# Normalized q and k transposed by a DMA from SBUF to SBUF, in place of TensorE transposes and a PSUM copy

## The chip, the cores and the metric

The kernel runs on one core of one Trainium2 chip. A core has five engines that run side by side: TensorE (PE in the profile; its weight loads are listed as PEld), VectorE (DVE), ScalarE (ACT), GpSimd (POOL) and SyncE (SP). Each works through its own instructions in a fixed order and waits on semaphores for the others. Here SP does nothing but issue DMA transfers, which 16 DMA engines carry out. SBUF is the working memory with 128 partitions, PSUM the memory into which TensorE writes.

The metric is the device time of one execution in microseconds (us); lower is better.

## The reference

Cosine attention, followed by a highway layer on its output:

```python
batch, n_heads, seq, head_dim = (8, 12, 448, 64)      # d_model = 768

q_n = q / (np.linalg.norm(q, axis=-1, keepdims=True) + 1e-06)
k_n = k / (np.linalg.norm(k, axis=-1, keepdims=True) + 1e-06)
scores = np.matmul(q_n, k_n.transpose(0, 1, 3, 2)) / tau          # tau = 0.1
scores = scores - np.max(scores, axis=-1, keepdims=True)
attn = np.exp(scores)
attn = attn / (np.sum(attn, axis=-1, keepdims=True) + 1e-09)
attn_out = np.matmul(attn, v)

x = attn_out.transpose(0, 2, 1, 3).reshape(B * S, H * D)          # 3584 x 768
H = np.maximum(x @ w_h, 0.0)
T = 1.0 / (1.0 + np.exp(-(x @ w_t + b_t)))
out = T * H + (1.0 - T) * x
```

## The kernel before

Work is cut into 8 batches of 6 pairs of heads. A pair's 448 rows lie on 112 partitions in 4 chunks; `(b,pr)` below is batch b, pair pr. For a pair the steps are these.

- `emit_A` loads q and k (two transfers of 224 KB, SP), squares them on POOL (`qk_sq`, L97) and sums the squares on DVE (L104).
- `emit_rsqrt` makes the inverse norms `yy` on DVE with eleven small operations, for batch 0 pair by pair and later for a whole batch at once.
- `emit_B` multiplies q and k by them on POOL (`qkn`, two instructions, L152), transposes `qkn` so that the head dimension lies on the partitions (`qkT`, eight blocks on PE, L157), copies the result from PSUM to SBUF on DVE (`qkt`, L164), loads v, and casts it to fp16 on ACT into `vp` (L174), whose last column POOL sets (the memset, L173).
- `emit_qkt` computes the scores (`sT`, L186) from `qkt`, and ACT takes their exponentials (`expt`, L194).
- `emit_av`, for each head, multiplies by v (`u`, 16 matmuls, L208); DVE divides by the row sums (`rd`, `xbach`, L219 and L220).

The highway layer of the batch before is spread over the heads of the current one (`ffn_slot`): a transpose of x on PE (`xTp`, L234), the two products (`pt`, L255), and the elementwise end on ACT and DVE, with one store for each of 4 row chunks. The last batch's layer runs alone at the end.

The code is not run in the order in which it is written. A scheduler sets the order on each engine from the dependences and from the order of writing, which gives each step its priority; `tc.high_priority(offset=300)` moves a step ahead. In the written order `emit_A(b+1, ...)` stands in the first six heads of batch b and `emit_B(b+1, ...)` in the last six. All of batch 0's pairs and the loads of the weights come first.

What holds a step back besides its inputs is a free buffer: 7 for `qk_raw`, 4 each for `qkn`, `qkt`, `vp` and `expt`, 3 for `v_raw`, and 2 PSUM buffers, tagged `pb1`, which `qkT`, `u` and `xTp` share. The weights' fp32 buffer exists once, so the load of `w_t` waits until DVE has cast `w_h` (L76).

Of the kernel before, what the change touches and what calls it, by code (L numbers as in the profile page):

```python
# [10 lines left out]
FP16 = mybir.dt.float16  # L11
# [7 lines left out]
def kernel(  # L19
# [11 lines left out]
    nc = tc.nc  # L31

    B, NH, S, D = q.shape
    P = 112
    NC = S // P
# [14 lines left out]
    qt_p = ctx.enter_context(tc.tile_pool(name="qt", bufs=4))  # L50
# [9 lines left out]
    pb1_p = ctx.enter_context(tc.tile_pool(name="pb1pool", bufs=2, space=bass.MemoryType.PSUM))  # L60
    ffnp_p = ctx.enter_context(tc.tile_pool(name="ffnpool", bufs=2, space=bass.MemoryType.PSUM))

    ident = const.tile([P, P], FP16)
# [82 lines left out]
    def emit_B(b, pr):  # L146
        qk_raw = st.pop(("qk_raw", b, pr))
        rs = st["rs", b].rearrange("p (pr t c h) -> p pr t c h", pr=NPAIR, t=2, c=NC)
        qkn = qkn_p.tile([128, 2, NC, 2, D], FP16, name="qkn")
        for t in range(2):  # L150
            in1 = rs[:P, pr, t].unsqueeze(3).to_broadcast([P, NC, 2, D])
            nc.gpsimd.tensor_mul(qkn[:P, t], qk_raw[:P, t], in1)  # L152

        qkT = pb1_p.tile([128, 2, 512], FP16, name="qkT", tag="pb1")
        for t in range(2):
            for c in range(NC):
                nc.tensor.transpose(  # L157
                    qkT[:, t, c * P : (c + 1) * P],
                    qkn[:P, t, c],
                    ident[:P, :P],  # L160
                )
        qkt = qt_p.tile([128, 2, S], FP16, name="qkt")
        with tc.high_priority(offset=300):
            nc.vector.tensor_copy(qkt[:, :, :], qkT[:, :, 0:S])  # L164
        st["qkt", b, pr] = qkt

        v_raw = vraw_p.tile([128, NC, 2, D], FP32, name="v_raw")
        nc.sync.dma_start(
            v_raw[:P],
            v[b, 2 * pr : 2 * pr + 2].rearrange("h (p c) d -> p c h d", c=NC),  # L170
        )
        vp = vp_p.tile([128, NC, 2, D + 1], FP16, name="vp")
        nc.gpsimd.memset(vp[:P, :, :, D], 2.0)  # L173
        nc.scalar.copy(vp[:P, :, :, 0:D], v_raw[:P])  # L174
        st["vp", b, pr] = vp
# [139 lines left out]
    for pr in range(NPAIR):  # L315
        emit_A(0, pr)
        emit_rsqrt(0, prs=pr)
        emit_B(0, pr)
# [11 lines left out]
    for b in range(B):  # L330
        for h in range(NH):
            pr, hh = h // 2, h % 2
            if b + 1 < B and h < NPAIR:
                emit_A(b + 1, h)
            if hh == 0:
                for h2 in (h, h + 1):
                    st["expt", b, h2] = expt_p.tile([128, NC, S], FP16, name="expt")
                emit_qkt(b, pr, 0)
                emit_qkt(b, pr, 1)
            emit_av(b, h)  # L340
            if b >= 1:
                ffn_slot(b - 1, h)
            if b + 1 < B and h >= NPAIR:
                if h == NPAIR:
                    emit_rsqrt(b + 1)
                    new_batch_tiles(b + 1)
                emit_B(b + 1, h - NPAIR)
# [6 lines left out]
_INS = ['q', 'k', 'v', 'tau', 'moe_w_h', 'moe_w_t', 'moe_b_t']  # L354
_OUTS = [((3584, 768), 'float32')]
#: Inputs that are plain numbers.
_NUMBERS = {'tau': 0.10000000149011612}


# [26 lines left out]
```

## Time and profile before

| | us |
|---|---|
| median of 2 runs | 512.3 |
| lowest and highest | 511.74 and 512.85 |
| span of the profiled execution (first to last instruction) | 509.7 |
| the profiled execution's busy times: PE, DVE, ACT, POOL | 412.6, 314.3, 226.1, 201.7 |
| mean granted TensorE clock, as a share of full speed | 0.887 |

The busy times overlap, since the engines run side by side, so they don't add up to the span. A PE busy time counts from a matmul's start to its modelled end, with overlapping matmuls counted once. In rows of instructions the first number is the start in us from the span's start, the second the length, then engine, line, operation, the tile written and the tile read, shapes, count, and in brackets the idle time before and what ended it. In rows of groups the numbers after the bar are the busy time in us and the mean length in ns. The granted clock is what the throttle allowed TensorE.

### The profile page before, as it was taken

What the parts mean: (1) busy time and instruction counts of PE and PEld (TensorE: products, weight loads), DVE (VectorE), ACT (ScalarE), POOL (GpSimd) and SP (SyncE); (2) the same over time, 40 slices, a digit from 0 to 9 for tenths busy, and PEclk for the clock granted to TensorE, in tenths of its full rate; (3) what the DMA queues carried; (4) which work ended last, traced back from release to release, by engine and by line L of the source; (5) the groups of instructions that cost most, each with busy time, mean ns of one, the idle gap of its engine ahead of it and who ended that gap; (6) DMA issues with size and microseconds to landing.
All of it is one profiled execution on the core that took longest, in us unless ns stands there. A gap on an engine that the chain in (4) does not pass through costs nothing.

```text
span 509.7 us, 8460 instructions
## 1 busy us (share of the span) xinstructions
PE 412.6 (81%) x3328; PEld 286.6 (56%) x3328; DVE 314.3 (62%) x661; ACT 226.1 (44%) x305; POOL 201.7 (40%) x198
## 2 busy tenths in 40 slices
PE   0545945988776979889878999989887999899995
PEld 0114604766554656557655666657564767575774
DVE  3655465458277675666777494938685455453574
ACT  1321441346335453354453473454546455644511
POOL 3663296723924276337170833282517030000000
PEclk9999999999967797677898797959897899797999
DMA  9960695725553157415551554255231221000012
GB/s 173 224 167 1 211 192 105 147 57 129 109 117 81 39 131 140 100 46 113 142 110 45 132 123 103 62 118 138 70 74 46 64 65 46 27 28 28 29 55 81
DMA packets 137033, 49.31 MB, mean 97 GB/s; under 512 B 131873, under 2 KB 131873, under 8 KB 136994
## 3 DMA queue, kind: packets, MB, share of 16 engines
q1 hardware_dynamic: 136994, 48.77, 42.9%
q8 instruction: 26, 0.43, 0.4%
q14 instruction: 13, 0.11, 0.1%
HBM read 37.75 MB, written 11.01 MB: 96 GB/s over the span
## 4 chain that ended last, share of the span: by engine, by line
PE 53%; DVE 23%; ACT 5%; POOL 5%; SPq 5%; DMA 4%; issue 3%; POOLq 0%; ACTq 0%
PE pt L255 24%; PE u L208 15%; PE sT L186 9%; DVE outst L299 6%; DVE th1a L291 6%; DVE n L104 4%; PE qkT L157 4%; POOL qkn L152 3%; ACT expt L194 3%; SPq L92 3%; DMA qk_raw<-in_k_dram 3%; ACT tt L271 2%; DMA qk_raw<-in_q_dram 2%; POOL qk_sq L97 2%; DVE xTb L240 1%
## 5 line engine op out<-in xcount | busy, mean ns | idle before, releaser
L194 ACT ACTIVATE expt<-sT 112x896 f16<-112x896 f32 x192 | 166.7, 916 | 96.5 <-PE sT L186 77.7
L208 PEld LDWEIGHTS <-expt 112*112 112x112 f16 x1536 | 115.5, 158 | 40.1 <-issue 17.4
L208 PE MATMUL u<-vp,expt 112*112 112x65 f16 x1536 | 121.5, 238 | 12.9 <-DVE xbach L220 9.2
L255 PEld LDWEIGHTS <-xTb 128*112 128x112 f16 x768 | 101.8, 145 | 47.8 <-DVE xTb L240 15.0
L152 POOL TENSOR_TENSOR qkn<-qk_raw,yy 112x512 f16<-112x512 f32 x96 | 99.7, 1068 | 72.4 <-DVE yy L144 37.7
L186 PE MATMUL sT<-qkt 64*112 64x448 f16 x384 | 104.3, 437 | 26.3 <-ACT expt L194 25.6
L97 POOL TENSOR_TENSOR qk_sq<-qk_raw 112x1024 f16<-112x1024 f32 x48 | 96.3, 2013 | 29.5 <-DMA qk_raw<-in_k_dram 23.3
L255 PE MATMUL pt<-w_h_f,xTb 128*112 128x384 f16 x384 | 100.0, 402 | 5.4 <-DVE xTb L240 4.4
L174 ACT CAST vp<-v_raw 112x512 f16<-112x512 f32 x48 | 29.8, 621 | 118.8 <-PE u L208 78.8
L255 PE MATMUL pt<-w_t_f,xTb 128*112 128x384 f16 x384 | 77.2, 330 | 0.4 <-DVE hmx L274 0.3
L104 DVE TENSOR_REDUCE n<-qk_sq 112x16 f16<-112x1024 f16 x48 | 58.0, 1211 | 26.2 <-POOL qk_sq L97 26.2
L291 DVE SCALAR_TENSOR_TENSOR th1a<-tt,hmx 112x384 f16<-112x384 f16 x64 | 51.1, 798 | 33.2 <-ACT tt L271 33.2
L157 PE MATMUL qkT<-ident,qkn 112*128 112x112 f16 x384 | 35.5, 247 | 44.2 <-POOL qkn L152 40.9
L186 PEld LDWEIGHTS <-qkt 64*112 64x112 f16 x384 | 31.2, 140 | 62.3 <-issue 55.4
L173 POOL MEMSET vp<- 112x8 f16 x48 | 6.9, 149 | 147.4 <-PE u L208 147.4
L274 DVE SCALAR_TENSOR_TENSOR hmx<-pt,xbach 112x384 f16<-112x384 f32 x64 | 35.2, 553 | 39.2 <-PE pt L255 39.2
L271 ACT ACTIVATE tt<-pt 112x384 f16<-112x384 f32 x64 | 31.4, 491 | 62.6 <-PE pt L263 62.0
L157 PEld LDWEIGHTS <-qkn 112*128 112x128 f16 x384 | 28.5, 116 | 54.5 <-POOL qkn L152 45.7
L219 DVE RECIPROCAL rd<-u 112x4 f32<-112x4 f32 x96 | 17.2, 179 | 55.3 <-PE u L208 54.4
L299 DVE SCALAR_TENSOR_TENSOR outst<-xbach,th1a 112x384 f32<-112x384 f16 x64 | 49.2, 769 | 1.0
L164 DVE COPY qkt<-qkT 128x896 f16<-128x896 f16 x48 | 29.8, 620 | 21.1 <-PE qkT L157 11.8
L220 DVE SCALAR_TENSOR_TENSOR xbach<-u,rd 112x256 f16<-112x256 f32 x96 | 40.3, 421 | 1.9
(55 smaller groups left out, 116.8 us busy)
## 6 DMA issues: line engine op xcount, KB each, us to landing
qk_raw<-in_q_dram SPq DMA_DIRECT2D x48, 224.0 KB, 4.4
qk_raw<-in_k_dram SPq DMA_DIRECT2D x48, 224.0 KB, 4.4
v_raw<-in_v_dram SPq DMA_DIRECT2D x48, 224.0 KB, 3.4
out_dram<-outst SPq DMA_DIRECT2D x32, 336.0 KB, 2.8
w_raw<-in_moe_w_h_dram SPq DMA_DIRECT2D x1, 2304.0 KB, 10.8
w_raw<-in_moe_w_t_dram SPq DMA_DIRECT2D x1, 2304.0 KB, 8.7
bt_raw<-in_moe_b_t_dram SPq DMA_DIRECT2D x1, 3.0 KB
```

Of the source, the lines that this page charges most:

```text
L97: nc.gpsimd.tensor_mul(qk_sq[:P], qk_raw[:P], qk_raw[:P])
L104: nc.vector.reduce_sum(n2[:P, pr], qk_sq[:P], axis=AX.X)
L152: nc.gpsimd.tensor_mul(qkn[:P, t], qk_raw[:P, t], in1)
L157: nc.tensor.transpose(qkT[:, t, c * P : (c + 1) * P], qkn[:P, t, c], ident[:P, :P],)
L186: nc.tensor.matmul(sTs[hh][:P, jj, 0:S], lhsT=qkt[hh * D : (hh + 1) * D, 1, jc * P : (jc + 1) * P], rhs=qkt[hh * D : (hh + 1) * D, 0, 0:S] ...
L194: nc.scalar.activation(st["expt", b, 2 * pr + hh][:P, 2 * g : 2 * g + 2, :], sTs[hh][:P, :, 0:S], AF.Exp, scale=inv_tau,)
L208: nc.tensor.matmul(u[:P, ic, 0 : D + 1], lhsT=expt[:P, jc, ic * P : (ic + 1) * P], rhs=vp[:P, jc, hh], start=(jc == 0), stop=(jc == NC - 1),)
L220: nc.vector.scalar_tensor_tensor(out=xb[:P, pr, :, hh, :], in0=u[:P, :, 0:D], scalar=0.0, in1=rd[:P, :].unsqueeze(2).to_broadcast([P, NC, D]),
L255: nc.tensor.matmul(pt[:P, :], lhsT=xT[:, cc, ic * P : (ic + 1) * P], rhs=w_f[:, cc, mh * MH : (mh + 1) * MH], start=(cc == 0), stop=(cc == ...
L271: nc.scalar.activation(tt[:P, mh], pt[:P, :], AF.Tanh)
L291: nc.vector.scalar_tensor_tensor(out=th1a[:P, mh], in0=tt[:P, mh], scalar=1.0, in1=hmx[:P, mh], op0=ALU.add, op1=ALU.mult,)
L299: nc.vector.scalar_tensor_tensor(out=outst[:P, mh * MH : (mh + 1) * MH], in0=xg, scalar=2.0, in1=th1a[:P, mh], op0=ALU.mult, op1=ALU.add,)
```

## The change

The eight PE transposes of a pair, their PSUM tile and the DVE copy are replaced by one DMA transpose, issued by SP. It reads `qkn` (112 partitions of 1024 fp16 values) and writes `qkt` (128 partitions of 8 blocks of 112), the same values in the same places. The buffer counts stay. `qkT` no longer takes a `pb1` buffer.

```diff
-        qkT = pb1_p.tile([128, 2, 512], FP16, name="qkT", tag="pb1")
-        for t in range(2):
-            for c in range(NC):
-                nc.tensor.transpose(
-                    qkT[:, t, c * P : (c + 1) * P],
-                    qkn[:P, t, c],
-                    ident[:P, :P],
-                )
-        qkt = qt_p.tile([128, 2, S], FP16, name="qkt")
-        with tc.high_priority(offset=300):
-            nc.vector.tensor_copy(qkt[:, :, :], qkT[:, :, 0:S])
+        qkt = qt_p.tile([128, 2 * NC, P], FP16, name="qkt")
+        nc.sync.dma_start_transpose(
+            qkt[:, :, :], qkn[:P].rearrange("p t c h d -> p (t c h d)")
+        )
+        qkt = qkt.rearrange("p (t c) s -> p t (c s)", t=2)
```

The scheduler then puts other things in another order too. Lines behind the edit have numbers lower by 6.

SP, in the first stage, before: the last loads of batch 0, the weights, and the first loads of batch 1 (`qk_raw_307` is pair (0,5), `qk_raw_359` is (1,0), `qk_raw_404` is (1,1)).

```order
L92 DMA qk_raw_307<-in_k_dram 112x8x64
L168 DMA v_raw_340<-in_v_dram 112x8x64
L73 DMA w_raw_345<-in_moe_w_h_dram 128x6x768
L79 DMA bt_raw_351<-in_moe_b_t_dram 1x768
L92 DMA qk_raw_359<-in_q_dram 112x8x64
L92 DMA qk_raw_359<-in_k_dram 112x8x64
L92 DMA qk_raw_404<-in_q_dram 112x8x64
L73 DMA w_raw_348<-in_moe_w_t_dram 128x6x768
```

And now (`qk_raw_262` is pair (0,5), `qk_raw_305` is (1,0); `qkt_226`, `qkt_255` and `qkt_284` are (0,3), (0,4) and (0,5)):

```order
L92 DMA qk_raw_262<-in_q_dram 112x8x64
L155 DMA_TRANSPOSE qkt_226<-qkn_223 128x8x112
L92 DMA qk_raw_262<-in_k_dram 112x8x64
L162 DMA v_raw_286<-in_v_dram 112x8x64
L73 DMA w_raw_291<-in_moe_w_h_dram 128x6x768
L155 DMA_TRANSPOSE qkt_255<-qkn_252 128x8x112
L155 DMA_TRANSPOSE qkt_284<-qkn_281 128x8x112
L79 DMA bt_raw_297<-in_moe_b_t_dram 1x768
L92 DMA qk_raw_305<-in_q_dram 112x8x64
L73 DMA w_raw_294<-in_moe_w_t_dram 128x6x768
L92 DMA qk_raw_305<-in_k_dram 112x8x64
```

The last transposes of batch 0 stand ahead of the load of `w_t`; two loads that were ahead of it, k of (1,0) and q of (1,1), now come after it.

POOL, in the same stage, before (`qkn_250`, `qkn_288` and `qkn_326` are pairs (0,3), (0,4) and (0,5); `vp_304` and `vp_342` are (0,4) and (0,5), `vp_640` is (1,0)):

```order
L152 TENSOR_TENSOR qkn_250<-qk_raw_231,yy_122 112x512 x2
L97 TENSOR_TENSOR qk_sq_272<-qk_raw_269 112x1024
L97 TENSOR_TENSOR qk_sq_310<-qk_raw_307 112x1024
L152 TENSOR_TENSOR qkn_288<-qk_raw_269,yy_122 112x512 x2
L152 TENSOR_TENSOR qkn_326<-qk_raw_307,yy_122 112x512 x2
L173 MEMSET vp_304 112x8
L173 MEMSET vp_342 112x8
L173 MEMSET vp_640 112x8
```

And now (`qkn_223`, `qkn_252` and `qkn_281` are (0,3), (0,4) and (0,5); `vp_259` and `vp_288` are (0,4) and (0,5); `vp_577`, `vp_607`, `vp_655` and `vp_685` are (1,0) to (1,3)):

```order
L167 MEMSET vp_259 112x8
L152 TENSOR_TENSOR qkn_223<-qk_raw_204,yy_122 112x512 x2
L97 TENSOR_TENSOR qk_sq_236<-qk_raw_233 112x1024
L167 MEMSET vp_288 112x8
L167 MEMSET vp_577 112x8
L152 TENSOR_TENSOR qkn_252<-qk_raw_233,yy_122 112x512 x2
L97 TENSOR_TENSOR qk_sq_265<-qk_raw_262 112x1024
L167 MEMSET vp_607 112x8
L152 TENSOR_TENSOR qkn_281<-qk_raw_262,yy_122 112x512 x2
L167 MEMSET vp_655 112x8
L167 MEMSET vp_685 112x8
```

A memset of `vp` waits until `u` of the pair four before it is done; these now stand between the multiplications of `qkn`.

SP, in batch 1, before (`v_raw_1402`, `v_raw_1459` and `v_raw_1524` are loads of v for batch 2; `qk_raw_1593`, `qk_raw_1656` and `qk_raw_1690` are (3,0) to (3,2)):

```order
L168 DMA v_raw_1402<-in_v_dram 112x8x64
L168 DMA v_raw_1459<-in_v_dram 112x8x64
L92 DMA qk_raw_1593<-in_q_dram 112x8x64
L307 DMA out_0_dram<-outst_1181 112x768
L92 DMA qk_raw_1593<-in_k_dram 112x8x64
L92 DMA qk_raw_1656<-in_q_dram 112x8x64
L168 DMA v_raw_1524<-in_v_dram 112x8x64
L92 DMA qk_raw_1656<-in_k_dram 112x8x64
L92 DMA qk_raw_1690<-in_q_dram 112x8x64
```

And now (`qkt_1265` and `qkt_1313` are (2,2) and (2,3), `qkt_1369` and `qkt_1424` are (2,4) and (2,5); the loads of q and k are those of batch 3):

```order
L155 DMA_TRANSPOSE qkt_1265<-qkn_1262 128x8x112
L155 DMA_TRANSPOSE qkt_1313<-qkn_1310 128x8x112
L162 DMA v_raw_1426<-in_v_dram 112x8x64
L92 DMA qk_raw_1431<-in_q_dram 112x8x64
L92 DMA qk_raw_1431<-in_k_dram 112x8x64
L92 DMA qk_raw_1494<-in_q_dram 112x8x64
L301 DMA out_0_dram<-outst_1415 112x768
L155 DMA_TRANSPOSE qkt_1369<-qkn_1366 128x8x112
L92 DMA qk_raw_1494<-in_k_dram 112x8x64
L92 DMA qk_raw_1528<-in_q_dram 112x8x64
L92 DMA qk_raw_1528<-in_k_dram 112x8x64
L155 DMA_TRANSPOSE qkt_1424<-qkn_1421 128x8x112
```

The transposes of a batch stand among the loads of the batch after it and the stores of the batch before it. Each waits for its `qkn` and for the scores that last read its `qkt` buffer, four pairs earlier.

## The prediction

> **What bounds the kernel now.** I call one pair's transposition of q and k "T" (48 of them: 8 batches of 6 pairs of heads; T(1,0) is batch 1, pair 0). The first view is the page: the span, each engine's busy share, and the slices.
>
> ```profile
> span 509.7 us, 8460 instructions
> PE 412.6 (81%) x3328; PEld 286.6 (56%) x3328; DVE 314.3 (62%) x661; ACT 226.1 (44%) x305; POOL 201.7 (40%) x198
> PE   0545945988776979889878999989887999899995
> DMA  9960695725553157415551554255231221000012
> q1 hardware_dynamic: 136994, 48.77, 42.9%
> ```
>
> PE leads, but not from the start: in the first seven slices (89 us) it is often half idle, and the transfers are full there. So I cut the span at the first scores matmul (sT) of each batch, and asked for the busy time of each stretch.
>
> ```profile
> 19.20:87.50 68.30, 39.86 (x245) 23.29 (x244) 37.35 (x91) 23.91 (x29) 37.54 (x29) 1.00 0.65 144
> 87.50:156.00 68.50, 58.90 (x499) 42.60 (x498) 39.84 (x85) 29.14 (x40) 37.94 (x37) 0.90 0.56 113
> 156.00:220.60 64.60, 54.49 (x417) 38.06 (x416) 45.33 (x80) 28.08 (x39) 31.46 (x28) 0.76 0.43 94
> 220.60:277.90 57.30, 49.76 (x420) 34.89 (x418) 41.74 (x86) 27.95 (x39) 24.21 (x24) 0.85 0.42 96
> 277.90:330.80 52.90, 48.56 (x417) 34.09 (x416) 36.93 (x76) 27.82 (x39) 24.99 (x24) 0.87 0.45 105
> 330.80:384.20 53.40, 48.55 (x419) 33.69 (x416) 36.87 (x77) 28.27 (x39) 24.20 (x25) 0.87 0.41 96
> 384.20:434.90 50.70, 46.40 (x418) 32.86 (x416) 27.56 (x60) 27.86 (x39) 12.76 (x17) 0.90 0.20 55
> 434.90:485.00 50.10, 46.23 (x384) 32.03 (x381) 23.67 (x57) 25.98 (x35) 0.27 (x2) 0.86 0.10 29
> 485.00:509.70 24.70, 18.18 (x116) 14.05 (x116) 14.89 (x29) 3.92 (x8) 0.00 (x0) 0.96 0.23 70
> ```
>
> After the length come the busy times of PE, PEld, DVE, ACT and POOL, the granted clock, the DMA share and GB/s. From batch 1 on PE is busy in 84 to 92% of each stretch, so these are PE's. Batch 7 (434.90 to 485.00) matters most: no T is left in it, POOL does next to nothing, and it still takes 50.1 us. No batch gets much below that by losing its T's.
>
> **What is removed.** The same view, of the transposes alone (PE and PEld busy), from batch 1 to batch 6:
>
> ```profile
> 87.50:156.00 68.50, 7.68 (x80) 6.61 (x80) 0.90 0.56 113
> 156.00:220.60 64.60, 4.45 (x49) 3.97 (x48) 0.76 0.43 94
> 220.60:277.90 57.30, 3.80 (x50) 3.27 (x48) 0.85 0.42 96
> 277.90:330.80 52.90, 3.67 (x49) 3.26 (x48) 0.87 0.45 105
> 330.80:384.20 53.40, 3.75 (x51) 3.27 (x48) 0.87 0.41 96
> 384.20:434.90 50.70, 3.32 (x50) 2.90 (x48) 0.90 0.20 55
> L164 DVE COPY qkt<-qkT 128x896 f16<-128x896 f16 x48 | 29.8, 620 | 21.1 <-PE qkT L157 11.8 <-PE sT L186 9.0
> ```
>
> Batches 2 to 6 lose 4.45 + 3.80 + 3.67 + 3.75 + 3.32 = 19.0 us of PE. I count all of it, since PE sets these stretches. Bounds: 0, if the holes fill with waits for ACT and DVE instead; 28.4, the sum of the five lengths (278.9) less five times 50.1. I stay at 19.0, between the two. The 48 copies of 0.62 us on DVE and the PSUM buffers that qkT shared with u and xTp count zero: DVE is busy 36.9 of 52.9 us in batch 4, and batch 7, where it is busy for only 23.7, is hardly shorter than batch 6. Should they free PE earlier, that lies inside the 28.4.
>
> **Batch 1.** PE in program order, around its start:
>
> ```profile
> 82.13 0.56 PE L157 MATMUL qkT<-ident,qkn 112*128 112x112 f16 x4 [10.02 <-POOL qkn L152]
> 83.47 1.67 PE L208 MATMUL u<-vp,expt 112*112 112x65 f16 x16
> 89.46 1.71 PE L208 MATMUL u<-vp,expt 112*112 112x65 f16 x16
> 92.76 1.70 PE L208 MATMUL u<-vp,expt 112*112 112x65 f16 x16
> 96.82 1.71 PE L208 MATMUL u<-vp,expt 112*112 112x65 f16 x16 [0.69 <-DVE xbach L220]
> ```
>
> PE stands 10.02 us at T(1,0), which waits for POOL's qkn, and batch 0's last five u groups are queued behind it. With no T in PE's queue they run in that hole. Three of them lie after 87.5 and leave batch 1: 1.71 + 1.70 + 1.71 = 5.1 us, and the T's of this stretch another 7.7. Together -12.8 us; bounds -5.1 (T's refilled) and -18.4 (down to 50.1).
>
> **The price of a T as a DMA.** The trace before holds none. The nearest rows are the loads, of the same 224 KB:
>
> ```profile
> qk_raw<-in_q_dram SPq DMA_DIRECT2D x48, 224.0 KB, 4.4
> v_raw<-in_v_dram SPq DMA_DIRECT2D x48, 224.0 KB, 3.4
> w_raw<-in_moe_w_h_dram SPq DMA_DIRECT2D x1, 2304.0 KB, 10.8
> ```
>
> From issue to landing I take 4.4 us, that of q with its equally short rows; the ends are 3.4 (v) and 10.8, the longest landing of the page. On the engines: 42.9% of 16 x 509.7 us over 136,994 packets is 25.5 ns each. A T reads 112 x 8 = 896 rows of 256 bytes, so 896 x 25.5 / 16 = 1.4 us of all 16 engines if the write side adds nothing. The built instruction cuts its source into tiles of 16 rows by 128 columns; were each transposed row of a tile (32 bytes) a packet, it is 7,168 and 11.4 us. I take the low end, because 224 KB is what a load moves at about that price, and keep 11.4 for the rival. By the Trainium skill (DMA: Bandwidth & Descriptors, "Latency and other measured facts") a DMA transpose has reached 261 GB/s; an estimate from it is 0.9 us for a T, and the sum stays as here; no run yet shows it.
>
> **The first stage.** SP now holds the T's in program order among the loads, and what is behind a waiting T waits too. The rows with the ends of the old chain:
>
> ```profile
> 17.57 2.04 POOL L152 TENSOR_TENSOR qkn<-qk_raw,yy 112x512 f16<-112x512 f32 x2 [1.15 <-DVE yy L144]
> 25.51 2.04 POOL L152 TENSOR_TENSOR qkn<-qk_raw,yy 112x512 f16<-112x512 f32 x2 [2.20 <-DVE yy L144]
> 20.85 1.72 ACT L194 ACTIVATE expt<-sT 112x896 f16<-112x896 f32 x2 [6.46 <-PE sT L186]
> 54.80 0.40 SPq L73 DMA_DIRECT2D w_raw<-in_moe_w_t_dram  x1
> 68.09 0.99 SPq L92 DMA_DIRECT2D qk_raw<-in_k_dram  x1
> 76.75 1.22 DVE L104 TENSOR_REDUCE n<-qk_sq 112x16 f16<-112x1024 f16 x1 [0.63 <-POOL qk_sq L97]
> ```
>
> In the new order POOL's memset for a vp buffer (which waits for a pair's u) stands ahead of the next qkn. So two pairs on: T 4.4, first sT and four exps 4.7 (row 20.85: 0.86 each), two u groups 3.4, then memset, rest of the square and two qkn about 3.8, together 16.3 us. T(0,2) leaves at about 27.5, when its qkn ended before (25.51 + 2.04). T(0,3) leaves at 35.3: POOL ends pair 2's qkn at 27.2 at the earliest and pair 3's square at 29.1, the reduction takes 1.2, DVE's small operations with pair 0's two xbach among them 3.0, two qkn 2.0. Hence T(0,4) at 43.8 and T(0,5) at 51.6. The load of w_t stands behind it, waits for DVE's cast of w_h at about the same time, and leaves at 53.5, against 54.80 before. Behind it are 11 loads of q and k where 9 were, 2 us more, so the last leaves at 53.5 + 13.3 + 2 = 68.8 against 68.09. From there as before, qkn of T(1,0) ends at 83.8 and 4.4 us later sT can start: 88.5 against 87.5, **+1.0**. T(0,3), T(0,5) and T(1,0) stand one behind another in this chain, so a microsecond more per T costs 3. Bounds: -3 at 3.4, +19 at 10.8.
>
> **Steady state.** A T must land before its sT, and SP must not be held up. The slack in batch 6:
>
> ```profile
> 374.33 0.61 DVE L164 COPY qkt<-qkT 128x896 f16<-128x896 f16 x1
> 384.20 0.59 PE L186 MATMUL sT<-qkt 64*112 64x448 f16 x4
> 337.14 0.68 SPq L92 DMA_DIRECT2D qk_raw<-in_k_dram  x1
> 383.83 8.30 POOL L152 TENSOR_TENSOR qkn<-qk_raw,yy 112x512 f16<-112x512 f32 x7
> ```
>
> The copy at 374.33 is T(6,2), which sT needs only two pairs after 384.20. A load of batch 7 leaves at 337.14 for a qkn after 383.83. So a T may be some 10 us late, and a load behind a waiting T some 40, before PE sees it: zero. That cover is gone only if a T takes over 10 us. SP's issues: 22 a batch at about 0.65 us, now 28, under 20 of 53 us: zero. Engines: loads and stores use 0.45 x 52.9 = 23.8 us of batch 4, six T's add 8.4: zero.
>
> **Sum.** +1.0 - 12.8 - 19.0 = -30.8, and the last stretch is unchanged. On the profiled span that is 478.9 us. The runs' median, 512.3, is 2.6 above the span, which I keep: **481.5 us**. Its own range is 463 (-3.0, -18.4 and -28.4) to 499 (+5, batch 1 -9, the others half of 19).
>
> **Rivals.**
> - *The transfers become the bound* (the other side). Batch 4 has 52.9 - 23.8 = 29.1 us of the engines free, 4.85 us for each of six T's; above that a batch is as long as its transfers. For it speaks the small size of what is written; against it, that loads of the same size leave 1.0 us apart. At 10.8 us a T, one after another with loads beside them, a batch is 64.8 us: 88.5 + 3 x 6.4 + 6 x 64.8 + 50.1 + 24.7 + 2.6 = 574. At 11.4 us on all engines, not shared with the loads, it is 68.4 + 23.8 = 92 us a batch, about 740. By the Trainium skill (VectorE: DVE Perf Modes, "The three transpose paths") one 128x128 block takes 1309 ns through the DMA against 390 on TensorE, and its rules prefer TensorE where PSUM will do; an estimate of eight blocks in a row is 10.5 us, which would make this rival true at about 562. The trace has only the TensorE side: 3.32 us for batch 6's six T's, 0.55 for eight blocks and so less than the page says.
> - *A T lands late but does not hold the engines*, 10.8 us like w_h. The first stage grows by 19: 501.
> - *PE's freed time refills.* Batch 7's 50.1 us speaks for it, batch 3's 57.3 against. Then the 19.0 fall away: 500.5.
>
> **Numbers.** Forecast 0.55, late but covered 0.13, refill 0.08, transfers bound 0.24. Range 463 to 560: it holds the first three cases (0.76) and the mildest of the last, up to about 10 us a T. Over 2% (10 us, about what a measurement of this kernel can tell) faster means under 502: 0.55 + 0.07 + 0.02 = 0.64; same 0.06 + 0.06 = 0.12; slower 0.24.
>
> **What would show it.** The DMA rows give T's landing (4.4; over 10 is the second rival) and the packets' share (42.9% of the old span, about 60% now if a T costs 1.4 us; above 90% in a batch's middle is the first rival). The first sT of batch 1 should start near 88 and PE's 10 us wait be gone; batch 1 should take about 56 us, batches 2 to 6 about 260 together; batch 7 and the tail should not change. The forecast is wrong if SP stays at a T's own issue for microseconds, if POOL's qkn waits for T's, or if sT waits for qkt after batch 0.

## The result, and the profile after

| | before | after |
|---|---|---|
| median, us (2 runs each, same series) | 512.3 | 476.7 |
| lowest and highest | 511.74, 512.85 | 474.41, 479.03 |
| ratio, with its 95% interval | | 0.930 [0.918, 0.941] |
| span of the profiled execution | 509.7 | 477.0 |

A second series (6 runs) gave 477.3 us and 0.929 [0.925, 0.933]. The change makes the kernel 7% faster. Here and below, runs more than 1.5% above a kernel's fastest are left out of the ratios, but not of the medians.

The page of the changed kernel: span, busy times, PE and DMA in 40 slices, packets with their share, and landing of a T (one pair's transposition).

```profile
span 477.0 us, 7704 instructions
PE 372.5 (78%) x2944; PEld 254.5 (53%) x2944; DVE 283.0 (59%) x613; ACT 225.2 (47%) x305; POOL 205.5 (43%) x198
PE   0388640298798989698987988698987988999995
DMA  9369299497369754956686857558565744211022
q1 hardware_dynamic: 181538, 59.79, 60.6%
qkt<-qkn SPq DMA_TRANSPOSE x48, 3.0
```

A T lands 3.0 us after its issue. It adds (181,538 - 136,994) / 48 = 928 packets, which at 60.6% of 16 x 477.0 us over all packets are 25.5 ns each, so 1.5 us of all 16 engines. That is near the 896 rows, not the 7,168 pieces of 32 bytes. The estimate of 10.5 us, eight times the price of one block in the Trainium skill (VectorE: DVE Perf Modes, "The three transpose paths"), does not hold here, as a whole T lands in 3.0. Nor is it as cheap as 0.9 us, the estimate from the Trainium skill (DMA: Bandwidth & Descriptors, "Latency and other measured facts").

The same cut as before, at the first scores matmul (sT) of batches 1 to 7; columns as before (length, busy PE, PEld, DVE, ACT, POOL, clock, DMA share, GB/s).

```profile
19.10:91.40 72.30, 37.02 (x241) 24.27 (x241) 33.62 (x92) 25.16 (x31) 36.32 (x31) 1.00 0.74 168
91.40:144.20 52.80, 46.31 (x370) 31.98 (x370) 33.93 (x66) 27.30 (x37) 30.27 (x29) 0.94 0.68 136
144.20:195.10 50.90, 45.26 (x371) 31.20 (x370) 35.11 (x70) 27.69 (x38) 26.80 (x26) 0.90 0.68 143
195.10:248.00 52.90, 46.04 (x371) 30.91 (x370) 33.35 (x70) 27.93 (x38) 26.71 (x26) 0.87 0.75 138
248.00:303.10 55.10, 43.98 (x371) 29.47 (x370) 33.38 (x72) 27.92 (x38) 28.76 (x26) 0.90 0.76 144
303.10:354.90 51.80, 47.81 (x369) 32.33 (x368) 34.18 (x69) 27.92 (x38) 23.92 (x24) 0.81 0.59 128
354.90:403.90 49.00, 42.66 (x369) 29.09 (x368) 32.41 (x69) 28.02 (x38) 23.88 (x23) 0.93 0.57 120
```

| | before | after | difference | forecast |
|---|---|---|---|---|
| first sT of batch 1 starts at | 87.5 | 91.4 | +3.9 | +1.0 |
| batch 1 | 68.5 | 52.8 | -15.7 | -12.8 |
| batches 2 to 6 | 278.9 | 259.7 | -19.2 | -19.0 |
| batch 7 and the last layer | 74.8 | 73.1 | -1.7 | 0 |
| span | 509.7 | 477.0 | -32.7 | -30.8 |

The sums agree, but the batches don't gain as their T's were busy: batch 2 lost 13.7 us (its T's were busy for 4.45), batches 4 to 6 together 1.1 (10.7). Batch 5 explains itself by its clock: at 0.81 PE was busy for 47.81 us, and in the second series for 43.30 at 0.92. So I take two numbers for batches 2 to 6: PE's idle time (length less busy), and busy time multiplied by the granted clock, which gives PE's work at full clock. They come from the rows of each kernel's stretches, cut at its own sT's.

| batches 2 to 6 | length | PE busy | idle | busy x clock |
|---|---|---|---|---|
| before | 278.9 | 247.8 | 31.1 | 210.0 |
| after | 259.7 | 225.8 | 33.9 | 198.8 |
| after, second series | 253.7 | 220.6 | 33.1 | 200.1 |

The transposes are worth 11.2 us at full clock, 13.2 at the old mean clock (210.0 / 247.8 = 0.847). The other 8.8 us of busy time are the clock, 0.880 now. Idle time rose by 2.8. The second series has the same work to 1.3 us, and a clock of 0.907, so the clock's share of the gain differs from run to run. That it rose does not: over whole executions it was recorded as 0.913 to 0.924 in all 8 runs of the changed kernel, and as 0.881 to 0.900 in the runs of the kernel before.

Batch 1 has another cause besides. This is PE in the changed kernel at its start (start, length, engine, line, operation, and in brackets the wait):

```profile
63.04 3.01 PE L202 MATMUL u<-vp,expt 112*112 112x65 f16 x30
91.40 0.99 PE L180 MATMUL sT<-qkt 64*112 64x448 f16 x4 [25.34 <-DMA qkt<-qkn]
...
101.78 0.59 PE L180 MATMUL sT<-qkt 64*112 64x448 f16 x4
```

All u groups of batch 0 are done by 66 us, and PE then stands idle for 25.34 us until T(1,0). The old hole is filled, as predicted, and a longer wait with nothing behind it stands there. Further, the same four matmuls take 0.99 us at 91.40 and 0.59 at 101.78: PE works at a lower rate at first, although the view says clock 1.00. The clock's record has its first entry at 100.6 us, and the view counts what lies ahead of it as 1.00. In the kernel before, the first entry is at 108.3 us, where 16 u matmuls go from 1.50 us (at 107.09) to 0.97 (at 109.42). So 138 matmuls of batch 1 ran at the low rate there, and 51 now:

```profile
87.50:108.25 20.75, 19.00 (x138) 13.44 (x138) 8.76 (x18) 8.25 (x10) 11.37 (x12) 1.00 0.68 131
91.40:100.60 9.20, 8.13 (x51) 5.60 (x51) 1.67 (x4) 3.56 (x4) 6.93 (x7) 1.00 0.81 153
```

The u groups and T's that left batch 1 did their work at this low rate (1.70 and 0.94 us each, where T's of batch 6 take 0.55), so they were worth more than their count.

### The profile page after: what moved, and what is told of

Its sections match the earlier page's. It is cut to its first block, busy times and chain, and to the rows that moved or that the text cites. A ratio compares the mean times of both kernels' runs of the same rounds, so it can differ in the third digit from the quotient of the medians.

```text
span 477.0 us, 7704 instructions
## 1 busy us (share of the span) xinstructions
PE 372.5 (78%) x2944; PEld 254.5 (53%) x2944; DVE 283.0 (59%) x613; ACT 225.2 (47%) x305; POOL 205.5 (43%) x198
## 2 busy tenths in 40 slices
DMA packets 181575, 60.28 MB, mean 126 GB/s; under 512 B 176417, under 2 KB 176417, under 8 KB 181538
## 3 DMA queue, kind: packets, MB, share of 16 engines
q1 hardware_dynamic: 181538, 59.79, 60.6%
## 4 chain that ended last, share of the span: by engine, by line
PE 39%; DVE 21%; POOL 11%; DMA 11%; SPq 6%; ACT 6%; issue 4%; POOLq 0%; ACTq 0%
PE pt L249 18%; PE u L202 11%; DMA qk_raw<-in_k_dram 9%; PE sT L180 8%; POOL qkn L152 6%; POOL qk_sq L97 5%; DVE th1a L285 5%; DVE n L104 5%; DVE outst L293 4%; SPq L92 4%; ACT expt L188 4%; DMA qkt<-qkn 2%; SPq L155 2%; DVE xTb L234 2%; ACT tt L265 1%
## 5 line engine op out<-in xcount | busy, mean ns | idle before, releaser
L180 PE MATMUL sT<-qkt 64*112 64x448 f16 x384 | 94.8, 412 | 71.1 <-DMA qkt<-qkn 47.6
L202 PEld LDWEIGHTS <-expt 112*112 112x112 f16 x1536 | 116.3, 156 | 39.2 <-issue 22.3
L249 PEld LDWEIGHTS <-xTb 128*112 128x112 f16 x768 | 99.7, 143 | 69.0 <-DVE xTb L234 25.2
L152 POOL TENSOR_TENSOR qkn<-qk_raw,yy 112x512 f16<-112x512 f32 x96 | 106.4, 1140 | 45.9 <-DVE yy L144 45.9
L202 PE MATMUL u<-vp,expt 112*112 112x65 f16 x1536 | 123.4, 237 | 2.5 <-DVE xbach L214 2.0
L97 POOL TENSOR_TENSOR qk_sq<-qk_raw 112x1024 f16<-112x1024 f32 x48 | 94.2, 1969 | 56.9 <-DMA qk_raw<-in_k_dram 55.4
L249 PE MATMUL pt<-w_h_f,xTb 128*112 128x384 f16 x384 | 97.5, 392 | 17.2 <-DVE xTb L234 16.7
L249 PE MATMUL pt<-w_t_f,xTb 128*112 128x384 f16 x384 | 80.6, 335 | 6.5 <-DVE hmx L268 6.3
L180 PEld LDWEIGHTS <-qkt 64*112 64x112 f16 x384 | 30.5, 137 | 103.2 <-issue 49.8
L234 DVE COPY xTb<-xTp 128x672 f16<-128x672 f16 x32 | 15.7, 495 | 12.1 <-PE xTp L228 12.0
L257 PE MATMUL pt<-bth,ones_row 128*112 128x384 f16 x64 | 21.1, 329 | 0.0
L228 PE MATMUL xTp<-ident,xbach 112*128 112x112 f16 x192 | 15.2, 218 | 1.6 <-DVE xbach L214 1.6
```

Source lines behind the costliest of these rows:

```text
L97: nc.gpsimd.tensor_mul(qk_sq[:P], qk_raw[:P], qk_raw[:P])
L180: nc.tensor.matmul(sTs[hh][:P, jj, 0:S], lhsT=qkt[hh * D : (hh + 1) * D, 1, jc * P : (jc + 1) * P], rhs=qkt[hh * D : (hh + 1) * D, 0, 0:S] ...
L202: nc.tensor.matmul(u[:P, ic, 0 : D + 1], lhsT=expt[:P, jc, ic * P : (ic + 1) * P], rhs=vp[:P, jc, hh], start=(jc == 0), stop=(jc == NC - 1),)
L249: nc.tensor.matmul(pt[:P, :], lhsT=xT[:, cc, ic * P : (ic + 1) * P], rhs=w_f[:, cc, mh * MH : (mh + 1) * MH], start=(cc == 0), stop=(cc == ...
```

## The experiments

Edits are shown against the changed kernel where nothing else is said. Ratios are to the kernel before, run on the same chip.

**Dead transposes that wait for nothing.** Is it PE's time?

```diff
+    dummy = const.tile([128, 128], FP16)
+    nc.vector.memset(dummy[:, :], 0.5)
...
+        qkT = pb1_p.tile([128, 2, 512], FP16, name="qkT", tag="pb1")
+        for t in range(2):
+            for c in range(NC):
+                nc.tensor.transpose(
+                    qkT[:, t, c * P : (c + 1) * P],
+                    dummy[:P, :],
+                    ident[:P, :P],
+                )
```

> The changed kernel plus dead work: eight PE transposes of a constant tile for each pair, into a PSUM buffer of the tag pb1 that nothing reads. PE spends the old transposes' time again and pb1 is shared again, but nothing waits for POOL's qkn and no DVE copy is added. Theory A (batches 1 to 6 are as long as PE's work, so what counts is the removed PE time): batch 1 gets back 7.7 us and batches 2 to 6 get back 19.0, so 476.7 + 26.7 = 503 us. Theory B (the gain came from PE's queue, which no longer stands behind a transposition that waits for POOL; the work behind it moved ahead into the hole, and where PE still has other waits the transposes' time refills): only a part of the 26.7 comes back, at most the 12.2 us of batches 1 and 2, so 480 to 489 us.

492.9 us, 0.965 [0.954, 0.977]: between the two, with about half of the gain gone. In batches 2 to 6 busy time times clock is back at 211.1, the level of the kernel before.

**Dead transposes of qkn.** The same with `qkn[:P, t, c]` in place of the constant.

> The changed kernel plus dead work: the eight old PE transposes of qkn for each pair, into a PSUM buffer of the tag pb1 that nothing reads. PE's queue again stands at each pair's qkn, in about the order of the kernel before; there is no DVE copy, and sT still reads what the DMA wrote. Theory A (PE time alone): the same as with transposes that wait for nothing, 503 us. Theory B (the wait in PE's queue): the 10 us hole at T(1,0) is back, with batch 0's last u groups behind it, and batches 1 and 2 are again 65 us and more; 505 to 515 us, and 15 us or more above the kernel whose dead transposes wait for nothing.

512.9 us, 1.003 [0.997, 1.010]: all of the gain is gone, with the DMA still used. PE in this kernel, and batch 1 of the constant's kernel and of this one:

```profile
87.18 0.55 PE L162 MATMUL qkT<-ident,qkn 112*128 112x112 f16 x4 [11.34 <-POOL qkn L152]
88.53 1.67 PE L210 MATMUL u<-vp,expt 112*112 112x65 f16 x16
```

```profile
93.10:150.50 57.40, 51.11 (x416) 35.93 (x416) 35.43 (x67) 27.58 (x38) 31.88 (x30) 0.80 0.69 129
```

```profile
93.30:158.00 64.70, 59.81 (x491) 41.81 (x490) 35.00 (x73) 29.08 (x40) 31.37 (x32) 0.92 0.68 127
```

The hole is back, 75 matmuls (u groups and T's) fall into batch 1 instead of before it, and batch 1 is 7.3 us longer. That is the wait in PE's queue. Of the 18.7 us between the two spans, 11.2 more lie in batches 2 to 6, without more work there (busy x clock is 208.4): the mean clock is 0.864 against 0.901 (+6.8 us busy) and idle time is 4.4 higher. So the two experiments do not split the gain cleanly into PE time and waiting.

**The whole old path as dead work**: as the last, and a DVE copy of `qkT` into a tile `dead` at high priority.

> The changed kernel plus the whole old path as dead work: the eight PE transposes of qkn for each pair and the DVE copy of 0.62 us (high priority, as before) into a tile that nothing reads. What it takes beyond the kernel with dead transposes of qkn alone (512.9 us, 1.003 of the kernel before) is the copies; what it takes beyond the kernel before is the DMA transposes. If copies and DMA both cost nothing, as the prediction had it: 510 to 514 us. If the 1.003 hides a gain from the missing copies and an equal loss from the DMA: 520 to 530 us.

508.3 us, 0.990 [0.986, 0.994]. This is below both expectations. The kernel does everything that the kernel before does, and 48 DMA transposes, and is not slower. So no net cost of the copies or of the DMA transposes is seen. That each costs nothing by itself is not shown: the order of work is another one, and the clock in batches 2 to 6 is 0.879 against 0.847.

**The DMA for batch 0 only, and for the others only** (a condition `b == 0` or `b >= 1` chooses between the two ways).

> DMA transposes for batch 0 only; batches 1 to 7 by PE and the DVE copy as before. The first stage was 3.9 us longer with the DMA. Both theories: batches 1 to 6 are as before, so 512 to 516 us. If it comes out below 508, the DMA for batch 0 brings something that neither theory has.

> Batch 0 by PE and the DVE copy as before; DMA transposes for batches 1 to 7. Both theories: nearly the whole gain is left, since it came from batch 1 on; the first stage has its old length, or less, so 470 to 478 us. If it comes out at 485 or more, taking batch 0's transposes out of PE's queue was needed for batch 1's gain.

516.9 us, 1.001 [0.994, 1.008], and 484.8 us, 0.949 [0.935, 0.962]. The first shows no change, as expected. The second has most of the gain, but lies above the upper edge of the 470 to 478 that were expected, just under the 485 named there. Its sT(1,0) starts only at 98.0 us. POOL there:

```profile
79.18 0.13 POOL L180 MEMSET vp<- 112x8 f16 x1 [5.69 <-PE u L215]
79.30 9.30 POOL L97 TENSOR_TENSOR qk_sq<-qk_raw 112x1024 f16<-112x1024 f32 x5
```

Five squares of batch 1 stand behind a memset that waits for batch 0's u, and batch 0 runs later where its transposes are PE's.

**PE transposes, but later in PE's order.** Against the kernel before: transposes and copy are split from `emit_B` and written one pair ahead of their scores, with 8 buffers for qkn.

```diff
-    qkn_p = ctx.enter_context(tc.tile_pool(name="qkn", bufs=4))
+    qkn_p = ctx.enter_context(tc.tile_pool(name="qkn", bufs=8))
...
                 emit_qkt(b, pr, 1)
+                if b >= 1 and pr + 1 < NPAIR:
+                    emit_T(b, pr + 1)
```

> The kernel before, without any DMA transpose: PE transposes and DVE copy stay, but from batch 1 on each pair's are written one pair ahead of its scores rather than in the batch before, and qkn has 8 buffers in place of 4, so that POOL can run ahead. PE's queue then stands no longer at qkn while work of the batch before is behind it. If half of the change's gain is the wait in PE's queue, about that half comes without the DMA: 490 to 498 us. Rival (only the PE time of the transposes counts, or the hole moves to another place): 508 to 515 us.

521.9 us, 1.017 [1.010, 1.023]: no gain, as the rival had it, but slower than its 508 to 515 too. PE at T(1,0):

```profile
76.00 3.01 PE L212 MATMUL u<-vp,expt 112*112 112x65 f16 x30
93.98 0.55 PE L171 MATMUL qkT<-ident,qkn 112*128 112x112 f16 x4 [14.97 <-POOL qkn L152]
```

All of batch 0's u groups are now ahead of the hole, as in the changed kernel, and batch 1 is shorter (60.3 us), but the first stage is 10 longer (sT at 97.5), and batches 2 to 6 take 288.5 at a mean clock of 0.837. The work at full clock, 211.1, is the old one. Taking the u groups out from behind PE's wait in this way brought no gain: the hole itself is longer (14.97 us against 10.02), and the first stage too.

**Each T twice**, the first into a scratch tile.

> Each DMA transpose is issued twice, the first into a scratch tile that nothing reads: 48 more transfers. If a second T costs the engines what the first did (928 packets, 1.5 us of all 16) and takes another 1.25 us of SP and some 1.5 us to land, the prediction's slopes give +4.5 us in the first stage (3 us per us of T) and nothing from batch 1 on, so 481 us, with the packets' share at 72 to 78% of the span. Rival (transfers are near to being the bound already): six more T's a batch lengthen batches 1 to 6 by 1.5 us each T, +9 us a batch, so 525 us or more.

499.9 us, 0.969 [0.965, 0.972]. sT(1,0) starts at 97.5, 6.1 us later than in the changed kernel. Of these, 1.6 are there at the very first sT (20.7 against 19.1), and 4.5 lie in the stage behind it (76.8 against 72.3), which is the forecast slope. From batch 1 on the forecast of nothing was wrong: PE now waits 2.7 to 5.8 us for a T at the start of each of batches 2 to 7. SP and PE at batch 2, and PE at batch 3:

```profile
147.97 1.25 SPq L155 DMA_TRANSPOSE twin<-qkn  x1
149.27 1.28 SPq L159 DMA_TRANSPOSE qkt<-qkn  x1
```

```profile
152.82 0.99 PE L184 MATMUL sT<-qkt 64*112 64x448 f16 x4 [5.30 <-DMA qkt<-qkn]
...
210.56 0.99 PE L184 MATMUL sT<-qkt 64*112 64x448 f16 x4 [5.83 <-DMA qkt<-qkn]
```

In batches 2 to 6 idle time is 47.4 against 33.9. T(b,0) leaves right after its qkn, and sT takes it at once. In the changed kernel T(2,0) to T(7,0) land 5.4 to 15.9 us ahead of their sT (issue plus 3.0): that is all the cover there is. Here T(2,0) lands 14.0 us later than there. The second issue is 1.3 of these, and the rest lies ahead of the T, on POOL (two rows of this kernel, then one of the changed one):

```profile
145.84 0.13 POOL L171 MEMSET vp<- 112x8 f16 x1 [6.47 <-PE u L206]
145.89 5.99 POOL L152 TENSOR_TENSOR qkn<-qk_raw,yy 112x512 f16<-112x512 f32 x5
...
133.38 4.67 POOL L152 TENSOR_TENSOR qkn<-qk_raw,yy 112x512 f16<-112x512 f32 x4 [5.68 <-DVE yy L144]
```

The qkn of batch 2 start 12.5 us later, where batch 1 had started 6.1 later, and they stand behind a memset that waits for a u. The same memset stands there in batches 3, 5 and 7, where PE's wait is 5.7 to 5.8 us. So the run prices a longer T in the first stage; behind it, most of what PE waits comes from a later qkn, and not from the second issue.

**8 buffers for qkt.** One number in the pool of `qkt`.

> 8 buffers for qkt in place of 4, so that a T no longer waits on SP for the scores of the pair four before it (58.8 us of waiting on SP in the changed kernel), and the loads behind it leave earlier. If a late load costs nothing, as the prediction had it: 474 to 479 us, no change. Rival (the loads behind waiting T's come too late for POOL's squares and DVE's sums, 55.4 us of waiting for k against 23.3 before, and that is why batches 4 to 6 gained only 1.1 us of the 10.7 that their T's took): batches 3 to 6 get down to 49 to 50 us, so 462 to 468 us.

480.0 to 494.3 us in four runs, median 488.9 (before: 513.9). No gain is seen, and the spread is too wide for a verdict. In the profiled run (480.0) batches 3 and 4 are down to 50.0 and 49.0 us, as the rival had it, but batches 1, 2 and 5 take 60.7, 54.3 and 54.3.

**The weights after batch 1's loads.** `emit_weights()` is called after the last `emit_A(1, ...)`.

> The loads of w_h and w_t are written after those of batch 1's q and k, so that these don't stand behind w_t, which waits for DVE's cast of w_h. If the first stage is set by the loads behind w_t (the last left at 74.7 us, T(1,0) at 88.4), sT(1,0) starts at 76 to 82 us in place of 91.4, and the whole is 462 to 468 us, if batch 1 doesn't wait for the weights. Rival: w_t then comes too late for batch 0's highway layer, which PE does within batch 1; the first stage's gain is lost in batch 1, and the whole stays at 474 to 479 us.

474.1 us, 0.918 [0.911, 0.924], the fastest kernel of this study; beside the changed one's 0.929 [0.925, 0.933] by about 1%. PE:

```profile
82.39 0.99 PE L180 MATMUL sT<-qkt 64*112 64x448 f16 x4 [17.77 <-DMA qkt<-qkn]
...
149.89 0.62 PE L180 MATMUL sT<-qkt 64*112 64x448 f16 x2 [10.64 <-DMA qkt<-qkn]
```

The first stage is 9 us shorter, so the loads behind w_t did set it. Batch 1 takes 67.5 in place of 52.8, and ends with a wait of 10.64 us for T(2,0). T(2,0) waits for its qkn, which POOL starts only at 144.80, since batch 2's squares stand there behind memsets that wait for u. Batch 1 is 14.7 us longer, so it gives back more than the first stage's 9. That is the rival's time, but not its way: PE has no wait for the weights in batch 1. The 1% comes from batches 2 to 6, which take 252.1 in place of 259.7, and from the end.

**Batch 1's norms pair by pair.** `emit_rsqrt(1, prs=pr)` before each `emit_B(1, pr)`.

> Batch 1's inverse norms are made pair by pair, as batch 0's are, in place of once for all six pairs: T(1,0) then waits for the load of its own pair alone, not for the last of the batch. DVE gets 55 more small operations. If PE's wait of 25.3 us at T(1,0) is what is left of the old wait, and it ends by the last load, sT(1,0) starts 5 to 12 us earlier and the whole is 465 to 472 us. Rival: T(1,0) still stands behind the last loads on SP or behind the squares on POOL, and nothing changes: 474 to 479 us.

488.9 us, 0.952 [0.946, 0.957]: slower than the changed kernel, by a way that neither expectation had. sT(1,0) starts at 80.1, 11 us earlier. Then DVE and PE:

```profile
76.09 0.99 DVE L125 CAST x32p<-n 112x16 f32<-112x16 f16 x1
77.11 1.82 DVE L126 TENSOR_SCALAR yy<-x32p 112x16 int32<-112x16 int32 x1
78.96 0.17 DVE L129 TENSOR_SCALAR yy<-yy 112x16 int32<-112x16 int32 x1
```

```profile
103.17 0.89 PE L249 MATMUL pt<-w_h_f,xTb 128*112 128x384 f16 x2 [18.34 <-DVE xTb L234]
```

The sums and norms of five pairs, 5.9 us each, stand on DVE ahead of the copy of xTb that the highway layer needs, and PE waits 18.34 us for it.

**q and k loaded by POOL's queue** (`nc.gpsimd.dma_start` in `emit_A`).

> The loads of q and k are issued by POOL in place of SP, so that they don't stand behind T's that wait for qkn; POOL gets 96 issues. In the changed kernel the last load of a batch, its square, its sum and the norms end only 5 to 16 us before the next batch's first sT needs T(b,0). If SP's order holds the loads back, the first stage shortens by 5 to 10 us and batches 1 to 3 by some us each: 460 to 470 us. Rival (POOL's issues cost POOL's own time on the same chain, where a load's price on POOL is not known from any run): 477 us or more.

506.5 to 519.8 us in four runs. POOL's issues cost it 81.5 us for k and 67.8 for q:

```profile
L92 POOL DMA_DIRECT2D qk_raw<-in_k_dram x48 | 81.5, 1698 | 0.0
L92 POOL DMA_DIRECT2D qk_raw<-in_q_dram x48 | 67.8, 1412 | 1.3 <-issue 0.8
```

The first sT of all starts at 34.4 in place of 19.1. What SP's order costs the loads cannot be read from this.

## Why the prediction was right, and where not

- *The price of a T.* 4.4 us was taken between 3.4 and 10.8; it is 3.0, below the lower end. 1.4 us of the engines was 1.5. The rivals on transfers, at 4.85 us of all engines a T, fall with it. That removed copies and added transfers count zero fits the whole old path as dead work (0.990), which shows no net cost of the two.
- *The first stage, +1.0.* It was +3.9, though T was 1.4 cheaper. (The forecast's own sum is a little off: 83.8 and 4.4 make 88.2, not 88.5.) T(0,5) left at 54.82 us (forecast 51.6). POOL and DVE there:

```profile
50.51 4.29 POOL L152 TENSOR_TENSOR qkn<-qk_raw,yy 112x512 f16<-112x512 f32 x2 [1.52 <-DVE yy L144]
```

```profile
50.34 2.55 DVE L76 CAST w_h_f<-w_raw 128x4608 f16<-128x4608 f32 x1
```

  qkn took 4.29 us in place of 2.04, since its first half stood still until DVE's cast ended. The forecast let that cast run beside it for nothing. w_t then left at 57.36 (53.5), and the loads behind it took 17.3 us (15.3), until 74.7. When T was doubled, the stage behind the first sT grew by 4.5 us, the forecast slope of 3 for some 1.5 us; the first sT itself was 1.6 later, which the slope left out.
- *Batch 1, -12.8.* It was -15.7 (-14.2 in the second series). The u groups moved into the hole as predicted, and the dead transposes of qkn, which bring the hole back, take them out again. What the forecast did not see is that PE's low rate ends earlier, after 9.2 us of batch 1 in place of 20.8.
- *Batches 2 to 6, -19.0.* It was -19.2, but the step "I count all of it, since PE sets these stretches" was right only in its sum. T's busy rows add up to 19.0, yet the work that left is 11.2 us at full clock, 13.2 at the old one. One reason lies in the reading: rows of neighbouring matmuls overlap, so a group's own busy time is more than PE gains when the group goes. Over the whole kernel before, the PE groups' busy times add up to 476.2 us, and PE is busy for 412.6. In the six kernels of the table below that do or repeat the transposes on PE, busy x clock is 208 to 212, in five without it 195 to 201 (the DMA for the others only has 199.8, the loads by POOL's queue 196.6). The rest came from the granted clock. Had it stayed at 0.847, this execution would be near 486. That 19.2 came out beside 19.0 is luck: it is 13.2 of work where 19.0 were counted, and 8.8 of clock that the forecast did not have, less 2.8 of idle time.

| batches 2 to 6 | clock | idle | busy x clock |
|---|---|---|---|
| before; DMA for batch 0 only | 0.847; 0.858 | 31.1; 30.5 | 210.0; 210.6 |
| later in PE's order | 0.837 | 36.2 | 211.1 |
| dead transposes: constant; qkn; with copy | 0.901; 0.864; 0.879 | 39.2; 43.6; 38.6 | 211.1; 208.4; 212.3 |
| after; weights later; norms by pair | 0.880; 0.885; 0.875 | 33.9; 26.7; 32.2 | 198.8; 199.4; 198.6 |
| 8 buffers; each T twice | 0.894; 0.842 | 33.0; 47.4 | 201.1; 194.6 |

- *Steady state, "zero".* True for one T, but the cover was far thinner than the forecast's "some 10 us" for a T: it was read at T(6,2), two pairs from its use, where T(b,0) is the one that counts. With each T issued twice it was gone, and PE waited 2.7 to 5.8 us at the starts of batches 2 to 7, in batch 2 mostly because its qkn came later from POOL.
- *Batch 7.* It was to stay; with the last layer it lost 1.7 us, at a clock of 0.89 against 0.85.
- *The refill.* No rival won, though idle time did rise by 2.8 us.

The forecast had no term for the granted clock, and the traces show what goes with it. It isn't the amount of PE work alone: the dead transposes with the copy do all of it and have 0.879. The clock's record has only two values, 1.00 and 0.50, and changes only in steps of 3.41 us. Cut at these steps, the 14 traces of this study have 1216 pieces at 1.00. Of the 844 in which PE was busy for at least 85%, none was followed by a piece at 0.50; of the 95 in which it was busy for less than 60%, 89 were. The clock went back to 1.00 177 times, 170 of them after a piece in which PE was busy for at least 95%, though 81 such pieces at 0.50 did not bring it back at once. Here is one such case in the changed kernel (columns as above; PE's busy time is the second number behind the stretch, the clock the third from the end):

```profile
114.23:117.64 3.41, 3.12 (x24) 2.16 (x23) 3.38 (x10) 1.18 (x3) 1.02 (x3) 1.00 1.07 216
117.64:121.05 3.41, 1.56 (x12) 0.72 (x11) 3.38 (x3) 3.25 (x4) 3.41 (x2) 1.00 0.01 3
121.05:124.46 3.41, 1.94 (x16) 1.79 (x17) 2.61 (x4) 0.00 (x0) 0.58 (x1) 0.50 0.43 118
124.46:127.88 3.42, 3.42 (x23) 2.79 (x22) 1.45 (x5) 0.00 (x0) 0.13 (x1) 0.50 0.86 185
127.88:131.29 3.41, 3.30 (x21) 1.85 (x20) 3.20 (x10) 1.96 (x3) 0.00 (x0) 1.00 0.03 4
```

So a wait of PE of a microsecond or two can be followed by several at half rate. In batches 2 to 6 the kernel before has 11 stretches at 0.50, together 85.3 us; the changed one has 8 with 61.4 us, and 9 with 47.8 in the second series. What stays open is which change in PE's short waits made them fewer, and whether the idle time sets the clock or only goes with it: no run changed the one and held the other.

## What to carry to other kernels

Before crediting an engine with the busy rows of what leaves it, multiply each stretch's busy time by the granted clock and keep its idle time apart: the product shows what work left, the idle time shows what was freed or newly waited for. Then look at what stands ahead of each drop of the clock: here short waits of PE did, so a wait may cost more than its own length. Judge the cover of a new transfer at its first use in a stage, not at a later one. And when a chain gets shorter at one place (weights later, norms earlier), look at which in-order queue the moved step now stands ahead of: here DVE's copy of xTb behind the earlier norms, and POOL's squares behind memsets that wait for u, gave it back.

## What the runs showed of the hardware

- PE's matmuls run at a low rate in the whole first stage, with the clock shown as 1.00: four sT take 0.99 us there and 0.59 at 101.78. In the kernel with constant dead transposes the record starts early and says 0.50 for the stretch 19.4 to 93.1, and an sT group takes 1.00 there as well, so the lower figure is the believable one. By the Trainium skill (TensorE: Matmul & The Clock Gate, "Part 1: The HAM clock gate (the "warmup" mystery)") the clock is halved until some microseconds of sustained activity release it. In the first stage the trace agrees with the halving (0.50), not with the time: before the change PE was busy for 19.00 of 20.75 us in batch 1 before its matmuls sped up. Later in the kernels it agrees better: in 170 of 177 cases the clock came back after 3.41 us with PE busy for at least 95%.
- From there on the granted clock is 1.00 or 0.50 and nothing between, and none of the 844 pieces of 3.41 us with PE busy for at least 85% was followed by 0.50, while 89 of the 95 below 60% were.
- POOL and DVE hold each other up. POOL's two qkn take 4.29 us together, the first of them 3.29 from 50.51, where each takes about 1.03 otherwise. A DVE cast beside it ends at 52.89. The other way, DVE's shift for `yy` (77.11 us, in the kernel with the norms pair by pair, above) takes 1.82 us, and its neighbour on as many values 0.17; it ends at 78.93, when POOL ends this:

```profile
77.00 1.90 POOL L97 TENSOR_TENSOR qk_sq<-qk_raw 112x1024 f16<-112x1024 f32 x1
```

  By the Trainium skill (SBUF — State Buffer, "SBUF: two separate sides") the two engines share a pair of ports, which for some kinds of DVE instruction one of them holds for a whole instruction; the trace agrees in both places.
- A DMA transpose costs SP 1.25 us to issue, about twice a load's 0.6 to 0.7 us.
